# Feed-forward parts of 2, 2, 4, 4, 4 and 2 token tiles instead of 2, 2, 2, 3, 3, 3 and 3 in a planned attention, feed-forward and expert kernel

## The chip, the core and the metric

One core of a Trainium2 chip runs the whole program. The metric is the device time of one execution in microseconds (us). The kernel before takes 813.25 us (median of three runs, 813.02 to 813.59).

## What is computed

2304 tokens (18 tiles of 128) of width 512 go through three layers:

```python
scores = scale * q @ k.T                       # 4 batches, 8 heads, 576 positions, width 64
attn   = softmax(where(0 <= i - j < 64, scores, -1e9))
x      = attn @ v                              # 2304 x 512
xn     = x / sqrt(mean(x*x) + 1e-6) * rms_g
x      = (silu(xn @ w_gate) * (xn @ w_val)) @ w_out       # d_ff 1536
logits = x @ w_gate2;  e = argmax(logits)                 # 8 experts
out    = softmax(logits)[e] * sigmoid(x @ w_output_gate)[e] * (relu(x @ w1[e]) @ w2[e])
```

All is float32. The large products are made of three: each operand is split into a rounded high part and the rest, and high x high, high x low and low x high are added up in one PSUM bank.

## The kernel before

**Parts and groups.** `SIZES` cuts the 18 token tiles into feed-forward parts. Parts 0 and 1 form the first group and run side by side; every later part is a group of its own. A group goes through the 12 chunks of d_ff (`ffn_step`, L968 on): for one chunk and one part, 12 matmuls make the gate (`gv`, L993 to L995, into one bank of 128 x 128 times the number of tiles), 12 make the value, ScalarE takes tanh of the gate (L1005), VectorE makes u from it and multiplies with the value (L1010, L1018), h is split into high and low (helpers at L452 and L459), and `mo` (L1035 to L1037) adds three matmuls over 512 columns to the accumulator of each tile. So a part of n tiles holds n of the eight PSUM banks from its first chunk to its last. `ffn_end` copies the accumulators out (L1051, L1053).

**What runs beside it.** Before a group, the attention of its tiles must be done (`attention_tile`: scores L680 and L688, maximum L707, exponentials L717, transposes L751, product with v L768, norm L795 to L845); their normed tokens go to `xn`, a room in SBUF of six tiles' size that the parts share by the offsets in `XN_AT`. In the first group the weights are converted too (`conv`: three loads, three splits per chunk) and written back to `whd` in DRAM (`save`); every later group keeps the four chunks that the one before it used last and loads the other eight from `whd` (L969). The buffers of tag `w` hold one chunk each: four are there from the start, five more when attention is over, one when the feed-forward layer is over.

**Routing and the first expert.** Behind each part, `route` transposes its tokens (L1103), makes the logits (L1110, L1118), picks the expert and the slot of every token, and POOL scatters the tokens by slot to `xs` in DRAM (L1199). After the last part but one `plan_first` counts the tokens of each expert so far (matmul L1274) and picks the fullest; its number (`idf`) tells SP which weights to load (L1415, to `raw`, then split to `w`) and which two tiles of its tokens (L1452, to `t2k`). They are transposed (L1469) and are the first expert block, which fills the time in which the last part is routed. Then come the eight experts in order of size (`experts`).

**What sets the order.** Every operation is given to `Plan` with its engines, a cost and a due time; `Plan.order` hands them out in a list schedule, by due time plus the entry of `SHIFT` for its place, and keeps slots of buffers and banks. The result is a fixed order for each engine: each runs its queue in order, and waits at an instruction whose inputs are not there. `K` holds the planner's constants. Where the plan sees TensorE waiting at the start, it puts small matmuls on a spare bank (`warm`, L624).

Of the kernel before, what the change touches and what calls it, by code (L numbers as in the profile page):

```python
# [10 lines left out]
F32R = mybir.dt.float32r  # L11
# [11 lines left out]
P = 128  # L23
# [7 lines left out]
SIZES = [2, 2, 2, 3, 3, 3, 3]  # L31
GROUPS = [[0, 1], [2], [3], [4], [5], [6]]
XN_AT = [0, 2, 4, 0, 3, 0, 3]
# [4 lines left out]
K = dict(  # L38
    w_r=4, sl=1.2, n_q=4, n_kt=4, n_s=4, n_m=4, n_p=4, n_x=4, n_y=3, n_xf=1, n_val=3, pf=0.1, cold=6.0, late=1, f0=24.0, pw=110.0, pb=0.6, c1a=0, c1v=0, spe=4, lact=0, warm=62.816, wf=1.644, flead=24.233, nwv=1, port=1.0, t0=46.214, pp=93.267,
    lead=1.781, clead=9.978, stag=2.552, stage=1.001, slack=-0.04, nt=2, look=-0.072, marg=-0.199, dw=1.739, ewl=3.278,  # L40
    ews=8.339, xld=43.407, xtn=7.222, mlead=14.712, vb=0.333, vb2=0.243, tb=22.485, share=-0.055, pls=9, phs=9, sf=0, hfs=1.431, stk=0.0, rlead=7.936, span=0.317, wl=1.841,
)
# [45 lines left out]
]  # L88


class Buf:


    def __init__(self, tag=None, t=None):
        self.tag, self.t, self.slot = tag, t, None
        self.last_w, self.reads = {}, {}
# [278 lines left out]
def attention_ffn_moe(  # L375
# [21 lines left out]
    KD = DM // P  # L397
# [220 lines left out]
    warm = []  # L618
# [1193 lines left out]
```

## Time and profile before

| | |
|---|---|
| median of three runs | 813.25 us |
| the profiled execution | 815.9 us |
| its span, first to last instruction | 813.9 us |
| TensorE (PE) busy | 798.6 us, 98% |
| weight loads (PEld) busy | 723.1 us, 89% |
| VectorE (DVE) busy | 471.1 us, 58% |
| ScalarE (ACT) busy | 355.0 us, 44% |
| GpSimd (POOL) busy | 59.6 us, 7% |
| moved by DMA | 146.12 MB, mean 180 GB/s |
| granted TensorE clock, mean | 0.997 of full |

A group of the profile is one line of the kernel, one engine and one shape: its count, its busy time, the mean of one, and how long the engine sat idle before it and for whom. Matmuls are pipelined, so the mean of one is longer than the distance from one start to the next; the timeline gives the starts. SP issues the DMAs; it is a queue of its own.

### The profile page before, as it was taken

What the parts mean: (1) busy time and instruction counts of PE and PEld (TensorE: products, weight loads), DVE (VectorE), ACT (ScalarE), POOL (GpSimd) and SP (SyncE); (2) the same over time, 40 slices, a digit from 0 to 9 for tenths busy, and PEclk for the clock granted to TensorE, in tenths of its full rate; (3) what the DMA queues carried; (4) which work ended last, traced back from release to release, by engine and by line L of the source; (5) the groups of instructions that cost most, each with busy time, mean ns of one, the idle gap of its engine ahead of it and who ended that gap; (6) DMA issues with size and microseconds to landing.
All of it is one profiled execution on the core that took longest, in us unless ns stands there. A gap on an engine that the chain in (4) does not pass through costs nothing.

```text
span 813.9 us, 15811 instructions
## 1 busy us (share of the span) xinstructions
PE 798.6 (98%) x6050; PEld 723.1 (89%) x6050; DVE 471.1 (58%) x1262; ACT 355.0 (44%) x993; POOL 59.6 (7%) x103
## 2 busy tenths in 40 slices
PE   9999999999999999999999999999999999999995
PEld 8899998889999998899999999898988799988893
DVE  6999998774554433852445334355466574666650
ACT  6988767664333323631523122223245333534530
POOL 2110000020000010200100101000100100110010
PEclk9999999999999999999999999999999999999998
DMA  8888899977335501642044904710295562756420
GB/s 303 281 270 292 302 287 332 293 255 269 126 130 188 188 26 53 247 146 87 2 156 162 362 33 143 234 52 1 78 330 174 188 205 91 227 188 227 152 83 21
DMA packets 53933, 146.12 MB, mean 180 GB/s; under 512 B 6800, under 2 KB 6800, under 8 KB 53856
## 3 DMA queue, kind: packets, MB, share of 16 engines
q1 hardware_dynamic: 50848, 135.36, 49.4%
q0 software_dynamic: 3008, 9.74, 3.1%
q8 instruction: 48, 0.79, 0.4%
q14 instruction: 29, 0.24, 0.1%
HBM read 120.66 MB, written 24.42 MB: 178 GB/s over the span
## 4 chain that ended last, share of the span: by engine, by line
PE 78%; issue 9%; DMA 6%; DVE 4%; SPq 1%; ACT 1%; POOL 0%; POOLq 0%; ACTq 0%; DVEq 0%
PE bank L993 11%; PE bank L995 10%; PE bank L994 10%; PE bank L1035 5%; PE bank L1036 5%; PE bank L1037 5%; PE bank L1538 3%; PE bank L1540 3%; PE bank L1539 3%; DMA raw<-in_moe_w_dram 3%; PE bank L1630 3%; PE bank L1632 3%; PE bank L1631 3%; PE bank L768 2%; PE bank L751 2%
## 5 line engine op out<-in xcount | busy, mean ns | idle before, releaser
L993 PE MATMUL bank<-xn,w 128*128 128x384 f32 (+1 forms) x672 | 215.2, 320 | 1.3 <-DVE u L1010 1.3
L995 PE MATMUL bank<-xn,w 128*128 128x384 f32 (+1 forms) x672 | 210.2, 313 | 0.0
L994 PE MATMUL bank<-xn,w 128*128 128x384 f32 (+1 forms) x672 | 210.1, 313 | 0.0
L993 PEld LDWEIGHTS bank<-xn,w 128*128 128x128 f32 x672 | 127.2, 189 | 6.2 <-DVE u L1010 1.7
L994 PEld LDWEIGHTS bank<-xn,w 128*128 128x128 f32 x672 | 127.1, 189 | 1.7
L995 PEld LDWEIGHTS bank<-xn,w 128*128 128x128 f32 x672 | 126.9, 189 | 0.0
L1010 DVE SCALAR_TENSOR_TENSOR u<-u,bank 128x384 f32<-128x384 f32 (+1 forms) x84 | 41.4, 494 | 88.4 <-ACT u L1005 88.0
L459 DVE TENSOR_TENSOR w<-raw,w 128x512 fp32r<-128x512 f32 x128 | 81.8, 684 | 10.5 <-ACT w L452 10.2
L1035 PE MATMUL bank<-wo,h 128*128 128x512 f32 x216 | 86.5, 401 | 0.0
L1036 PE MATMUL bank<-wo,h 128*128 128x512 f32 x216 | 84.8, 393 | 0.0
L1037 PE MATMUL bank<-wo,h 128*128 128x512 f32 x216 | 84.8, 392 | 0.0
L1005 ACT ACTIVATE u<-bank 128x384 f32<-128x384 f32 (+1 forms) x84 | 37.4, 447 | 95.6 <-PE bank L995 94.1
L452 ACT CAST h<-u 128x384 fp32r<-128x384 f32 (+1 forms) x73 | 34.2, 468 | 97.3 <-DVE u L1018 93.5
L1018 DVE TENSOR_TENSOR u<-u,bank 128x384 f32<-128x384 f32 (+1 forms) x84 | 41.5, 494 | 55.0 <-PE bank L995 53.8
L1538 PE MATMUL bank<-xT,w 128*128 128x256 f32 (+4 forms) x224 | 68.0, 304 | 1.5 <-DVE eh L1549 1.5
L1540 PE MATMUL bank<-xT,w 128*128 128x256 f32 (+4 forms) x224 | 67.3, 300 | 0.0
L1539 PE MATMUL bank<-xT,w 128*128 128x256 f32 (+4 forms) x224 | 67.2, 300 | 0.0
L452 ACT CAST w<-raw 128x512 fp32r<-128x512 f32 x85 | 48.8, 620 | 40.4 <-DMA raw<-in_moe_w_dram 16.8
L1630 PE MATMUL bank<-w,eh 128*128 128x512 f32 (+1 forms) x144 | 57.3, 398 | 0.0
L1544 ACT ACTIVATE eh<-bank 128x256 fp32r<-128x256 f32 (+4 forms) x64 | 26.2, 411 | 70.1 <-PE bank L1540 68.1
L1632 PE MATMUL bank<-w,eh 128*128 128x512 f32 (+1 forms) x144 | 56.7, 394 | 0.0
L1631 PE MATMUL bank<-w,eh 128*128 128x512 f32 (+1 forms) x144 | 56.7, 394 | 0.0
(234 smaller groups left out, 1363.6 us busy)
## 6 DMA issues: line engine op xcount, KB each, us to landing
w<-whd SPq DMA_DIRECT2D x80, 512.0 KB, 4.3
raw<-in_moe_w_dram SPq DMA_DIRECT2D x64, 512.0 KB, 5.1
whd<-w SPq DMA_DIRECT2D x24, 512.0 KB, 6.8
val<-in_v_dram SPq DMA_DIRECT2D x18, 512.0 KB, 3.3
kt<-in_k_dram SPq DMA_DIRECT2D x18, 384.0 KB, 6.6
raw<-in_moe_w_gate_dram SPq DMA_DIRECT2D x12, 512.0 KB, 5.0
raw<-in_moe_w_val_dram SPq DMA_DIRECT2D x12, 512.0 KB, 5.4
raw<-in_moe_w_out_dram SPq DMA_DIRECT2D x12, 512.0 KB, 5.9
```

The source lines that it names most:

```text
L452: nc.scalar.copy(o, i)
L459: ve[e].tensor_tensor(out=o, in0=i, in1=h, op=ALU.subtract)
L993: nc.tensor.matmul(o, lhsT=h_, rhs=xn.t[:, 0, kk], start=(kk == 0), stop=False)
L994: nc.tensor.matmul(o, lhsT=h_, rhs=xn.t[:, 1, kk], start=False, stop=False)
L995: nc.tensor.matmul(o, lhsT=l_, rhs=xn.t[:, 0, kk], start=False, stop=(kk == KD - 1))
L1035: nc.tensor.matmul(o, lhsT=h.t[:, 0, c], rhs=wo.t[:, 0, f], start=(n == 0), stop=False)
L1036: nc.tensor.matmul(o, lhsT=h.t[:, 0, c], rhs=wo.t[:, 1, f], start=False, stop=False)
L1037: nc.tensor.matmul(o, lhsT=h.t[:, 1, c], rhs=wo.t[:, 0, f], start=False, stop=(n == NF - 1))
L1538: nc.tensor.matmul(o, lhsT=wh, rhs=x.t[:, 0, kk, 0:N], start=(kk == 0), stop=False)
L1539: nc.tensor.matmul(o, lhsT=wh, rhs=x.t[:, 1, kk, 0:N], start=False, stop=False)
L1540: nc.tensor.matmul(o, lhsT=wl, rhs=x.t[:, 0, kk, 0:N], start=False, stop=(kk == KD - 1))
L1630: nc.tensor.matmul(bk.t[0:M], lhsT=hh, rhs=wh, start=(f == 0), stop=False)
```

## The change

The parts become 2, 2, 4, 4, 4 and 2 tiles. `xn` has room for eight tiles, so a part of four can be read while the next part's four are written. Buffers that are as wide as a part (u, h, the routing's small tables) grow to four tiles. To make room, the attention has three buffers for k, not four; of the `w` buffers one that came when attention was over now comes when the feed-forward layer is over, and `pln`, the table of the last planning step, also comes then. The planner's constants and all of `SHIFT` are new, so that the order of every engine is new. The instructions of attention, of the output projection and of the experts are as many as before.

```diff
-SIZES = [2, 2, 2, 3, 3, 3, 3]
-GROUPS = [[0, 1], [2], [3], [4], [5], [6]]
-XN_AT = [0, 2, 4, 0, 3, 0, 3]
+SIZES = [2, 2, 4, 4, 4, 2]
+GROUPS = [[0, 1], [2], [3], [4], [5]]
+XN_AT = [0, 2, 4, 0, 4, 0]
...
-    w_r=4, sl=1.2, n_q=4, n_kt=4, n_s=4, n_m=4, n_p=4, n_x=4, n_y=3, n_xf=1, n_val=3, pf=0.1, cold=6.0, late=1, f0=24.0, pw=110.0, pb=0.6, c1a=0, c1v=0, spe=4, lact=0, warm=62.816, wf=1.644, flead=24.233, nwv=1, port=1.0, t0=46.214, pp=93.267,
-    lead=1.781, clead=9.978, stag=2.552, stage=1.001, slack=-0.04, nt=2, look=-0.072, marg=-0.199, dw=1.739, ewl=3.278,
-    ews=8.339, xld=43.407, xtn=7.222, mlead=14.712, vb=0.333, vb2=0.243, tb=22.485, share=-0.055, pls=9, phs=9, sf=0, hfs=1.431, stk=0.0, rlead=7.936, span=0.317, wl=1.841,
+    w_r=4, sl=1.2, n_q=4, n_kt=3, n_s=4, n_m=4, n_p=4, n_x=4, n_y=3, n_xf=1, n_val=3, pf=0.1, cold=6.0, late=1, f0=24.0, pw=110.0, pb=0.6, c1a=0, c1v=0, spe=4, lact=0, warm=50.376, wf=2.323, flead=24.233, nwv=1, port=1.0, t0=46.214, pp=93.267,
+    lead=1.781, clead=9.978, stag=2.552, stage=1.001, slack=0.09, nt=2, look=-0.944, marg=0.033, dw=1.502, ewl=3.278,
+    ews=8.339, xld=43.407, xtn=7.222, mlead=14.712, vb=0.26, vb2=0.734, tb=240.248, share=-0.025, pls=9, phs=9, sf=0, hfs=1.431, stk=0.053, rlead=7.936, span=0.317, wl=1.841,
...
-    27.9, 32.5, -30.4, -6.6, -30.9, -2.2, 14.9, -18.9, -29.4, -12.2, -14, -10.2, -17.3, 2.2, -8.6, -67.2, -20, -17.8, -1.6, 1.1, 15.8, 14.7, -22.3, 1.4,
+    -24.3, -39.7, -60.5, -75.7, -59.5, -9.2, -7.3, -36.3, -37.3, -23.9, -37.4, -1.9, -62.3, -24.9, -3.3, -8.4, 16.3, -40, -9.7, -14.7, -26.9, -2.8, -47.7, -76.8,
...
-    tag("w", [("r", K["w_r"]), ("mr", 9 - K["w_r"]), ("ml", 1)], 0, [P, 2, 2, KD, P], F32R)
+    tag("w", [("r", K["w_r"]), ("mr", 8 - K["w_r"]), ("ml", 2)], 0, [P, 2, 2, KD, P], F32R)
     tag("fx", "mr", 1, [P, 2, KD, FIRST * P], F32R)
-    tag("pln", "mr", 1, [1, 1024])
+    tag("pln", "ml", 1, [1, 1024])
...
-    xn_all = fp.tile([P, 6 * 2 * KD * P], F32R, name="xn", bufs=1)
+    xn_all = fp.tile([P, 8 * 2 * KD * P], F32R, name="xn", bufs=1)
```

Two lines fewer in the tables make every line of the functions two smaller: L993 before is L991 now.

**TensorE, inside a part of three tiles before and of four now.** The last three matmuls of a value group and the first three of the output projection, before:

```order
L993 MATMUL bank_3908<-xn,w_3808 128x384
L994 MATMUL bank_3908<-xn,w_3808 128x384
L995 MATMUL bank_3908<-xn,w_3808 128x384
L1035 MATMUL bank_3818<-wo,h_3874 128x512
L1036 MATMUL bank_3818<-wo,h_3874 128x512
L1037 MATMUL bank_3818<-wo,h_3874 128x512
```

and now:

```order
L991 MATMUL bank_3415<-xn,w_3152 128x512
L992 MATMUL bank_3415<-xn,w_3152 128x512
L993 MATMUL bank_3415<-xn,w_3152 128x512
L1033 MATMUL bank_3333<-wo,h_3382 128x512
L1034 MATMUL bank_3333<-wo,h_3382 128x512
L1035 MATMUL bank_3333<-wo,h_3382 128x512
```

Each gate or value matmul streams 512 columns where it streamed 384; over all parts these lines have 576 matmuls each instead of 672, 288 of them over 512 columns. The warm-up matmuls of L624 are 258 instead of 248.

**TensorE, where the tokens of the first expert block (`t2k`) are transposed.** Before, behind the last output matmuls of the last part:

```order
L1035 MATMUL bank_6366<-wo,h_6908 128x512
L1036 MATMUL bank_6366<-wo,h_6908 128x512
L1037 MATMUL bank_6366<-wo,h_6908 128x512
L1469 MATMUL bank_6944<-ident,t2k_6568 128x128 x4
L1469 MATMUL bank_6954<-ident,t2k_6547 128x128 x4
L1103 MATMUL bank_6961<-ident,raw_6950 128x128 x4
L1103 MATMUL bank_6971<-ident,raw_6952 128x128 x4
```

and now, inside the last part:

```order
L1033 MATMUL bank_5896<-wo,h_6270 128x512
L1034 MATMUL bank_5896<-wo,h_6270 128x512
L1035 MATMUL bank_5896<-wo,h_6270 128x512
L1467 MATMUL bank_6348<-ident,t2k_6285 128x128 x4
L991 MATMUL bank_6356<-xn,w_5873 128x256
L992 MATMUL bank_6356<-xn,w_5873 128x256
L993 MATMUL bank_6356<-xn,w_5873 128x256
```

The transposes of the first tile moved from behind the last chunk to a place with nine gate and value groups of the part behind them. Between the count (L1274 before, L1272 now) and this place the new order has 96 gate and value matmuls over 256 columns and 24 output matmuls.

**SP, the first loads for the first expert block.** `raw` are weights, `t2k` tokens. Before:

```order
L1392 TENSOR_LOAD idf
L1415 ISA
L1415 DMA raw_6539<-in_moe_w_dram 128x2x512
L1392 TENSOR_LOAD idf
L1452 ISA
L1452 DMA t2k_6547<-xs 128x514
L1415 ISA
L1415 DMA raw_6566<-in_moe_w_dram 128x2x512
L1392 TENSOR_LOAD idf
L1452 ISA
L1452 DMA t2k_6568<-xs 128x514
```

and now:

```order
L1413 DMA raw_6239<-in_moe_w_dram 128x2x512
L1413 ISA
L1413 DMA raw_6251<-in_moe_w_dram 128x2x512
L1413 ISA
L1413 DMA raw_6267<-in_moe_w_dram 128x2x512
L1390 TENSOR_LOAD idf
L1450 ISA
L1450 DMA t2k_6285<-xs 128x514
L1390 TENSOR_LOAD idf
L1450 ISA
L1450 DMA t2k_6306<-xs 128x514
```

Three weight loads stand ahead of the first token load where one stood. VectorE's first weight cast of this block reads the third load now (`raw_6267`), the fifth before, and stands with four steps of the last part to come, not six.

## Rows read from the trace of the kernel before

**Rows 1.** The page: span, TensorE's share, and the granted clock in 40 slices.
```profile
span 813.9 us, 15811 instructions
...
PE 798.6 (98%) x6050; PEld 723.1 (89%) x6050; DVE 471.1 (58%) x1262; ACT 355.0 (44%) x993; POOL 59.6 (7%) x103
...
PEclk9999999999999999999999999999999999999998
```

**Rows 2.** TensorE's waits: operation <- releaser: us in total, times, longest.
```profile
PE bank L1538 <- DVE eh L1549: 1.5, 2, 1.1
PE bank L993 <- DVE u L1010: 1.3, 1, 1.3
PE warm L624 <- DVE ones_b L535: 1.2, 1, 1.2
```

**Rows 3.** The timeline, TensorE, the last matmul: start, us.
```profile
804.60 0.40 PE L1632 MATMUL bank<-w,eh 128*64 128x512 f32 x1
```

**Rows 4.** TensorE's groups by shape: count, busy us, mean ns, idle before.
```profile
L993 PE MATMUL bank<-xn,w 128*128 128x384 f32 x384 | 131.5, 342 | 1.3 <-DVE u L1010 1.3
...
L624 PE MATMUL warm<-ones_b 128*128 128x128 bf16 x248 | 18.5, 234 | 1.2 <-DVE ones_b L535 1.2
```

**Rows 5.** The timeline, TensorE: first and next start of four runs of matmuls.
```profile
61.93 0.28 PE L993 MATMUL bank<-xn,w 128*128 128x256 f32 x1
...
64.81 1.03 PE L751 MATMUL bank<-ident,s 128*128 128x128 f32 x8
...
250.30 0.33 PE L993 MATMUL bank<-xn,w 128*128 128x384 f32 x1
...
254.49 1.03 PE L1103 MATMUL bank<-ident,raw 128*128 128x128 f32 x8
...
543.77 0.40 PE L1035 MATMUL bank<-wo,h 128*128 128x512 f32 x1
...
547.89 0.34 PE L993 MATMUL bank<-xn,w 128*128 128x384 f32 x1
...
777.63 0.39 PE L1631 MATMUL bank<-w,eh 128*128 128x512 f32 x1
...
782.99 0.25 PE L1538 MATMUL bank<-xT,w 128*128 128x192 f32 x1
```

**Rows 6.** The page's DMA issues: the weight reloads, KB each, us to landing.
```profile
w<-whd SPq DMA_DIRECT2D x80, 512.0 KB, 4.3
```

**Rows 7.** Busy time by stretch: length, PE, PEld, DVE, ACT, POOL, clock, DMA share, GB/s.
```profile
46.00:100.00 54.00, 53.84 (x460) 49.95 (x459) 50.67 (x127) 45.27 (x118) 2.08 (x2) 1.00 0.87 285
100.00:160.00 60.00, 60.00 (x515) 54.88 (x513) 52.19 (x128) 40.34 (x108) 1.04 (x1) 1.00 0.96 302
...
200.00:300.00 100.00, 100.00 (x728) 92.30 (x726) 47.02 (x127) 34.47 (x114) 3.14 (x5) 1.00 0.41 146
```

**Rows 8.** VectorE's and ScalarE's groups: four that come with every attention tile.
```profile
L707 DVE TENSOR_REDUCE m<-bank 128x4 f32<-128x512 f32 x36 | 23.5, 681 | 6.1 <-PE bank L688 6.1
...
L717 ACT ACTIVATE s<-bank,m 128x128 f32<-128x128 f32 x144 | 50.9, 379 | 0.5
...
L717 ACT ACTIVATION_READ_ACCUMULATOR s<-bank,m 128x1 f32 x144 | 31.6, 219 | 0.0
...
L452 ACT COPY p<-bank 128x512 f32<-128x512 f32 x30 | 17.2, 591 | 11.4 <-PE bank L751 11.2
```

**Rows 9.** The timeline, 500 to 530 us: count, scatters, loads, first cast.
```profile
502.45 0.18 PE L1274 MATMUL bank<-pf,ones_b 128*128 128x8 bf16 x1
...
504.52 0.97 POOL L1199 DMA_INDIRECT xs<-raw,si  x1 [48.42 <-issue]
...
505.80 0.98 POOL L1199 DMA_INDIRECT xs<-raw,si  x1 [0.22 <-issue]
...
512.54 0.40 SPq L1415 DMA_DIRECT2D raw<-in_moe_w_dram  x1
513.56 0.35 SPq L1452 DMA_DIRECT2D t2k<-xs  x1
...
517.93 0.15 DVE L1462 COPY meta<-t2k 128x1 int32<-128x1 int32 x1 [1.51 <-DMA t2k<-xs]
...
526.49 0.43 DVE L456 CAST w<-raw 128x512 fp32r<-128x512 f32 x1 [3.14 <-DMA raw<-in_moe_w_dram]
```

80 rows, old and new, of the table SHIFT are left out of this document.

## The prediction

> **What bounds the kernel.** I read the page's first two parts, then TensorE's own waits, then its groups by shape, then its pace in the timeline, then the stretches in which another engine could stop it. The profiled execution took 815.9 us, its span 813.9 us; the median of the runs is 813.25 us, 2.65 us less. The sum below is made against 815.9 and then moved by that 2.65.
>
> In [rows 1] TensorE (PE) is busy for 98% of the span and its granted clock stands at 9 tenths or more in every slice but the last. In [rows 2] everything that ever stopped it for over 1 us is 1.5 us in the expert blocks (L1538, two waits), 1.3 us in the last feed-forward part (L993, one wait) and the start (L624). The last matmul starts at 804.60 us [rows 3]; the 9.3 us behind it are the last output tile and stay. So the time is the number of matmuls times their pace, plus stalls. A change of the parts pays only if TensorE streams its columns in less time, or waits less.
>
> **The change, part by part.**
>
> *Gate and value matmuls.* The three-tile parts issue 1152 matmuls over 384 columns, 384 on each of three lines [rows 4]. The change issues 864 over 512 columns: three parts of four tiles, 12 chunks, 2 x 12 matmuls each. The busy means there (342 ns) overlap, so the price is the distance of starts [rows 5]. At 384 columns 24 matmuls take 254.49 - 250.30 = 4.19 us, 0.1746 each; 1152 of them are 201.1 us. At 512 columns there is none of this line, but the output projection has that shape: 18 from 543.77 to 547.89 give 0.2289, and the expert layer's 23 from 777.63 to 782.99 give 0.2330. 864 of them are 197.8 to 201.3 us; I take the middle, 199.6 (0.231 each). **Gain 1.5 us, between 3.3 us and a loss of 0.2 us.** The gain is small because 384 and 512 columns cost 0.455 and 0.451 ns a column. The Trainium skill (TensorE: Matmul & The Clock Gate, section "Back-to-back issue gap") gives columns over 2.4 GHz plus about 2.5 ns for a matmul. By it I estimate 187.2 us for the old and 186.5 us for the new, a gain of 0.7 us. The rows are 12 to 17 ns above that rule at the two widths, so the measured paces stand. The output projection (648 matmuls) and the 864 matmuls at 256 columns stay as many.
>
> *Warm-up matmuls.* 248 now, 258 then; 18.5 us over 248 is 0.075 us each [rows 4], so 10 more are 0.75 us if they lengthen the start, 0 if they stand in a wait that is there anyway. The order places them only while TensorE waits for the first attention tiles. I take +0.4, bounds 0 and +0.75.
>
> *One part fewer.* 72 steps, not 84, on VectorE and ScalarE, and one routing round fewer: beside TensorE's matmuls, so nothing, whatever it saves.
>
> *Weight reloads.* 80 becomes 64 loads of 512 KB [rows 6]. They run in stretches where the DMA engines are busy for 0.41 of the time [rows 7]; nothing waits for them, so their loss brings nothing. If that cover went, one costs 4.3 us to land.
>
> *Two attention tiles more beside the first group.* The part behind the first group has four tiles, not two, so two tiles move from later into the weight conversion. TensorE's work for them is only moved. VectorE and ScalarE are the danger: from 46 to 160 us they are busy for 102.9 and 85.6 of 114 us, and TensorE still idles for only 0.16 us of them [rows 7]. A tile brings them at least 6.8 us: the four groups of [rows 8] are 123.2 us over 18 tiles. Two tiles are 13.7 us into 39.5 us of free time of the two engines. It fits, if it is spread; if it all fell on one engine half of it, 6.9 us, could show. Nearest row: the idle 0.16 us at that load. I take +0.4, bounds 0 and +6.9. Their loads (q, k, v) are also pulled forward, into DMA shares of 0.87 and 0.96 [rows 7]; that is in the same bound.
>
> *The last part and the first expert block.* Here the order moves most. Before, the last part has 12 steps of three tiles; the expert that goes first is counted early in it (matmul L1274, 502.45 us), SP then loads weights and tokens, and VectorE's first weight cast waits for its load until 526.49 us, 24.0 us after the count [rows 9]. VectorE runs in order; the u operation of the next step is queued behind that cast, and this is the 1.3 us of [rows 2]. That wait is tied to that place, which is gone: **-1.3 us** (bounds -1.3 and 0).
>
> In its place: in the new order PE comes to the first transpose of the first block's tokens inside the last part, with steps still behind it, where it stood after the last step. Between the count and that transpose stand 8 groups of 12 at 256 columns and four half-steps of 6 output matmuls; with 0.120 us (24 from 61.93 to 64.81, [rows 5]) and 0.231 us that is 11.5 + 5.5 = 17.0 us. The tokens come through the chain count, slot numbers, scatter on POOL, its landing, SP's load. Before, the first token tile is there at 517.93 us, 15.5 us after the count [rows 9]. In the new order three weight loads stand ahead of it on SP, not one; a place is 512.54 to 513.56 = 1.02 us, so +2.0. Four tiles are scattered, not three; one is 504.52 to 505.80 = 1.28 us, hidden or not. It lands 17.5 to 18.8 us after the count, 0.5 to 1.8 us after TensorE wants it; all steps left wait behind it in TensorE's queue. I take **+1.2 us**, bounds 0 (TensorE itself late) and +7.0 (the 24.0 us of the cast, less 17.0).
>
> *The rest planned anew.* The 1.5 us in the expert blocks are a matter of the order; 0, bounds -1.5 and +1.5.
>
> **Sum:** -1.5 + 0.4 + 0.4 - 1.3 + 1.2 + 0 = -0.8 us: 815.1 us for the profiled execution, **812.4 us** for the median. A difference under 0.2% (1.6 us) cannot be told from none by a measurement of this kernel.
>
> **Rivals.**
> 1. *Faster, 808 us.* The pace comes out at its lower bound, and the new order meets neither the old waits nor the new one: -3.3 + 0 + 0 - 1.3 + 0 - 1.5 = -6.1 us, 807.2 us. For it: 512 columns at 0.2289 are in the rows. Against: the other 512-column row is 0.2330, and the tokens' chain is measured. 0.20, for 807 to 811.
> 2. *Slower: the last part waits for the first expert block.* Place: the token transpose and the first weight cast in the last part. Price: from 3 to 7 us above the sum. It decides when the first token tile lands later than 20 us after the count, or the first cast holds VectorE with the u and h operations behind it (7 groups and 18 output matmuls, 14.3 us, stand between the count and that place). For it: the cast took 24.0 us before. Against: it then waited for the fifth weight load, now for the third. 815.4 to 819.4 us, 0.18.
> 3. *Slower: the first group runs out of VectorE and ScalarE*, up to 6.9 us, 816 to 819 us. 0.08; the rows speak for room.
> 4. *The clock falls.* With four accumulators TensorE has only four banks left to turn over in three parts. In the trace the first group already works so, and the granted clock is 1.00 there, 2.4 GHz [rows 7]. At 1.2 GHz every wide matmul would take 0.46 instead of 0.23 us, so 30 us at that level cost 15 us: 828 us. The Trainium skill (same page, section "A second HAM failure mode: psum-queue depth-cycling") tells of a kernel whose cycling through banks made the clock swing. By that rule the time would be that of this rival; the trace disagrees so far. 0.02.
> 5. *The start gets shorter*, 809 to 811 us, by some of the 18.5 us of warm-up. Against it: there are more of them, not fewer. 0.04.
>
> **How the numbers follow.** The forecast has 0.48, as 811.0 to 814.0 us; about 0.11 of that is below 811.6. Faster: 0.11 + 0.20 + 0.04 = 0.35. Within 0.2%: 0.37. Slower: 0.18 + 0.08 + 0.02 = 0.28. The range 808.5 to 818.5 us cuts a part of rival 1 and the top of rivals 2 and 3, and leaves out rival 4.
>
> **What would show it.** Right: 288 matmuls over 512 columns on each gate and value line, 24 of them in 5.5 to 5.6 us; no wait on L993 behind a weight cast over 1 us; a wait on the token transpose in the last part of 0.5 to 2 us on DMA; PE 98% busy. Wrong if TensorE idles by over 3 us in the last part (rival 2), or waits for u or a weight in the first group (rival 3), or if PEclk shows a slice under 9 (rival 4); and the pace is wrong if 24 wide matmuls take less than 5.4 us or more than 5.7 us.

## The result, and the profile after

The changed kernel takes 805.06 us (median of five runs, 804.04 to 807.94) where the kernel before takes 813.25: ratio 0.9898, 95% interval 0.9877 to 0.9918. It is faster by 8.2 us, 1.0%; the prediction was 812.4 us, and its range began at 808.5. Its profiled execution took 805.13 us, its span 803.3. Later comparisons gave 0.988 and 0.989.

The page of the changed kernel, first two parts:

```profile
span 803.3 us, 15138 instructions
...
PE 790.4 (98%) x5770; PEld 685.6 (85%) x5770; DVE 444.4 (55%) x1158; ACT 368.1 (46%) x1004; POOL 71.6 (9%) x117
...
PEclk9999999999999999999999999999999999999998
```

Beside [rows 1] the share of TensorE is the same 98% and the clock is as high; what fell is the busy time itself. The kernel was bound by TensorE and still is; it has less to stream. Its last matmul starts at 793.88 us (804.60 in [rows 3]), so the 9.4 us behind it are what they were, and all of the gain lies ahead of it.

TensorE's groups by shape and its longest waits:

```profile
L991 PE MATMUL bank<-xn,w 128*128 128x512 f32 x288 | 115.3, 400 | 0.0
...
L991 PE MATMUL bank<-xn,w 128*128 128x256 f32 x288 | 83.2, 289 | 0.6 <-DVE u L1016 0.6
...
L622 PE MATMUL warm<-ones_b 128*128 128x128 bf16 x258 | 19.3, 233 | 1.2 <-DVE ones_b L533 1.2
```

```profile
PE warm L622 <- DVE ones_b L533: 1.2, 1, 1.2
PE bank L843 <- DVE m L727: 1.1, 1, 1.1
PE bank L991 <- DVE u L1016: 0.6, 1, 0.6
```

The 288 wide matmuls a line are there. Of the two long waits of [rows 2], the expert layer's is gone and the last part's is shorter. The timeline of TensorE inside a part of four tiles, first matmul of a group and the start 24 matmuls later, and the last matmul of all:

```profile
196.38 0.39 PE L991 MATMUL bank<-xn,w 128*128 128x512 f32 x1
...
201.82 0.39 PE L991 MATMUL bank<-xn,w 128*128 128x512 f32 x1
...
793.88 0.40 PE L1630 MATMUL bank<-w,eh 128*64 128x512 f32 x1
```

24 matmuls (12 of a gate, 12 of a value) in 5.44 us: 0.2267 us each, where the prediction took 0.231 and named 5.5 to 5.6 us as the sign of being right. Of its other signs, the 98% came and no wait stands behind a weight cast; the wait on the token transpose did not come.

Where the time went is best seen by adding up, over a whole trace, the distance from each matmul's start to the next one's, shape by shape. A distance up to 45 ns above the median of its shape I count whole as streaming. Of a longer one the median counts as streaming and the rest as a hitch (45 to 130 ns over the median) or a wait (more). What the hitches are the traces do not tell. In us:

| trace | streaming | hitches | waits | sum |
|---|---|---|---|---|
| before | 750.7 | 33.3 | 19.4 | 803.4 |
| before, second trace | 750.9 | 33.5 | 17.9 | 802.3 |
| changed | 745.7 | 31.7 | 15.3 | 792.7 |
| changed, second trace | 745.1 | 32.8 | 15.3 | 793.2 |
| changed, third trace | 745.7 | 32.2 | 14.6 | 792.4 |

Streaming repeats within 0.6 us from one execution to the next. Means of these rows: 5.3 us less streaming, 1.2 less in hitches, 3.6 less in waits, 10.1 in all (the executions traced of before, 815.9 and 814.7 us, lie 2.65 and 1.45 us above the median of 813.25, so this is 1.9 more than the 8.2 of the medians). Of the streaming, the wide gate and value matmuls gave 3.5 (200.6 to 197.1), the output projection, whose instructions did not change, 1.3 (149.3 to 148.0), the second expert matmuls 0.6 (99.8 to 99.2).

### The profile page after: what moved, and what is told of

Read it like the earlier page. It is cut to its first block, busy times and chain, and to the rows that moved or that the text cites. A ratio compares the mean times of both kernels' runs of the same rounds, so it can differ in the third digit from the quotient of the medians.

```text
span 803.3 us, 15138 instructions
## 1 busy us (share of the span) xinstructions
PE 790.4 (98%) x5770; PEld 685.6 (85%) x5770; DVE 444.4 (55%) x1158; ACT 368.1 (46%) x1004; POOL 71.6 (9%) x117
## 5 line engine op out<-in xcount | busy, mean ns | idle before, releaser
L991 PE MATMUL bank<-xn,w 128*128 128x256 f32 (+1 forms) x576 | 198.5, 345 | 0.6 <-DVE u L1016 0.6
L993 PE MATMUL bank<-xn,w 128*128 128x256 f32 (+1 forms) x576 | 193.9, 337 | 0.0
L992 PE MATMUL bank<-xn,w 128*128 128x256 f32 (+1 forms) x576 | 193.7, 336 | 0.0
L991 PEld LDWEIGHTS bank<-xn,w 128*128 128x128 f32 x576 | 109.0, 189 | 14.1 <-issue 0.8
L993 PEld LDWEIGHTS bank<-xn,w 128*128 128x128 f32 x576 | 108.9, 189 | 11.7
L992 PEld LDWEIGHTS bank<-xn,w 128*128 128x128 f32 x576 | 109.1, 189 | 11.2
L1008 DVE SCALAR_TENSOR_TENSOR u<-u,bank 128x256 f32<-128x256 f32 (+1 forms) x72 | 39.5, 550 | 89.1 <-ACT u L1003 88.8
L450 ACT CAST h<-u 128x512 fp32r<-128x512 f32 (+1 forms) x65 | 34.0, 522 | 105.4 <-DVE u L1016 104.9
L1016 DVE TENSOR_TENSOR u<-u,bank 128x256 f32<-128x256 f32 (+1 forms) x72 | 39.7, 551 | 74.2 <-PE bank L993 73.1
L1003 ACT ACTIVATE u<-bank 128x256 f32<-128x256 f32 (+1 forms) x72 | 35.4, 492 | 96.5 <-PE bank L993 95.6
L450 ACT CAST w<-raw 128x512 fp32r<-128x512 f32 x99 | 56.2, 619 | 23.7 <-DMA raw<-in_moe_w_dram 11.8
L457 DVE TENSOR_TENSOR h<-u,h 128x256 fp32r<-128x256 f32 (+1 forms) x72 | 40.4, 561 | 23.9 <-ACT h L450 23.4
```

The source lines that it names most:

```text
L450: nc.scalar.copy(o, i)
L457: ve[e].tensor_tensor(out=o, in0=i, in1=h, op=ALU.subtract)
L991: nc.tensor.matmul(o, lhsT=h_, rhs=xn.t[:, 0, kk], start=(kk == 0), stop=False)
L992: nc.tensor.matmul(o, lhsT=h_, rhs=xn.t[:, 1, kk], start=False, stop=False)
L993: nc.tensor.matmul(o, lhsT=l_, rhs=xn.t[:, 0, kk], start=False, stop=(kk == KD - 1))
```

## The experiments

Each stands beside runs of the kernel before on the same chip.

**Both kernels once more.** No edit.

> The kernel before, unchanged, profiled once more. If the waits of its first trace belong to its order, the two longest (1.47 us on the gate matmul in the last part, 1.25 us on the expert weights) come again within 0.3 us, and all waits of TensorE over 0.13 us add up to 18 to 20 us. If they were chance of that execution (its 815.9 us stood 2.65 us over the median), one of the two is gone, the sum is 16 to 18 us and the span 811 to 812 us. The output matmuls over 512 columns: 0.231 us again if their pace is a matter of the kernel, 0.227 if of the execution.

> The changed kernel, unchanged, profiled and timed once more. If its gain is a matter of the kernel: ratio 0.988 to 0.992, 24 gate matmuls over 512 columns in 5.4 to 5.5 us, waits over 0.13 us of 15 to 16 us in all, no wait on the token transpose of the last part. If the first trace was a lucky one: a ratio over 0.993 and more waits.

Measured: before 814.7 us (span 812.8); changed 805.71, ratio 0.9884 (0.9851 to 0.9917). TensorE's waits in the second trace of before, and then of the changed kernel:

```profile
PE bank L993 <- DVE u L1010: 0.9, 1, 0.9
...
PE bank L1538 <- DVE eh L1549: 0.2, 1, 0.2
```

```profile
PE warm L622 <- DVE ones_b L533: 1.2, 1, 1.2
PE bank L1033 <- ACT h L450: 1.2, 1, 1.2
```

Of the two longest waits of [rows 2], the one behind the weight cast (1.3 us) is 0.9 us now and the one in the expert blocks (1.5 us) is 0.2: partly chance. And the changed kernel has a wait in its last part too, now on the output matmul (1.2 us, and 1.3 in the third trace; the gate wait of 0.6 us above is not there). TensorE waits there for h, and VectorE, which makes u for it, had waited 3.1 us for ScalarE's tanh. ScalarE's timeline at this tanh, first and second trace of the changed kernel:

```profile
530.22 0.38 ACT L1003 ACTIVATE u<-bank 128x256 f32<-128x256 f32 x1 [1.12 <-PE bank L993]
```

```profile
532.09 0.38 ACT L1003 ACTIVATE u<-bank 128x256 f32<-128x256 f32 x1 [3.14 <-PE bank L993]
```

The gate matmuls that it reads ended at 530.12 and 529.97 us. So the tanh followed after 0.1 us in one execution and after 2.1 us in the other, in the same order; why is not shown. Both median paces of the output matmuls, 0.231 and 0.227, came again: they belong to the kernels.

**The parts alone, in an order that nobody shaped.** `SHIFT` emptied in both, so that the planner's own order stands.

```diff
-SHIFT = [ -24.3, ...
+SHIFT = []
-    n_q=4
+    n_q=3
 # and, in parts3_plain alone
-SIZES = [2, 2, 4, 4, 4, 2]
+SIZES = [2, 2, 2, 3, 3, 3, 3]
-XN_AT = [0, 2, 4, 0, 4, 0]
+XN_AT = [0, 2, 4, 0, 3, 0, 3]
```

> The changed kernel with its table of shifts emptied (the planner's own order) and three q buffers, not four, so that its buffers fit. To be set against parts3_plain, which differs from it in the parts alone. Theory A (a fixed cost per matmul, so 288 fewer matmuls are worth something in any order): the 864 matmuls over 512 columns start 0.227 us apart, 3 to 4 us less in all than the 1152 over 384 columns of the other. Rival B (the order chosen by the shifts gives the pace): 0.231 us apart, and no difference of over 1 us in these matmuls. In both the waits grow, so the whole is 815 to 850 us; the sum of waits says how much of that is the order's.

> The same as parts4_plain (changed kernel's planner constants and buffers, room for eight tiles, table of shifts emptied, three q buffers), but with the parts of before: 2, 2, 2, 3, 3, 3, 3. Theory A: its gate and value matmuls over 384 columns take 0.173 to 0.175 us each, 200 to 201 us for 1152 without waits, 3 to 4 us more than the wide ones; output matmuls 0.229 to 0.231. Rival B: no difference of over 1 us. If it takes fewer waits than parts4_plain, the wide parts need the new order to be worth their gain; then the two times differ by less than 3 us or the other way round.

Measured: parts of four 817.86 us, ratio 1.0038 (1.0022 to 1.0054); parts of three 822.26, ratio 1.0093 (1.006 to 1.0127): 4.4 us apart.

| trace | streaming | hitches | waits | sum |
|---|---|---|---|---|
| parts3_plain | 755.1 | 31.5 | 22.7 | 809.4 |
| parts4_plain | 750.0 | 31.7 | 24.5 | 806.2 |

The difference in streaming is 5.1 us, nearly the 5.3 between the two kernels: gate and value 200.7 to 197.1, output 149.7 to 148.3. Theory A holds and the rival with the order falls. The wide parts do not wait less by themselves (1.8 us more here); that leaves the order for the fewer waits of the changed kernel.

**The wide matmuls cut in two.** The changed kernel, each gate and value group of a four-tile part done in two halves of 256 columns.

```diff
+            for c in (slice(0, 2 * P), slice(2 * P, 4 * P))[:PT // 2]:
             for kk in range(KD):
-                o = bk.t[:, 0:TW]
-                nc.tensor.matmul(o, lhsT=h_, rhs=xn.t[:, 0, kk], ...
+                o = bk.t[:, c]
+                nc.tensor.matmul(o, lhsT=h_, rhs=xn.t[:, 0, kk, c], ...
```

> The changed kernel, same parts and same order, but every gate or value matmul over 512 columns is issued as two over 256 (first all 12 of the left half, then all 12 of the right). Theory A (a fixed cost of 13 to 14 ns per matmul above columns over 2.4 GHz): 1728 matmuls at 0.1195 us are 206.5 us where the 864 took 197.1, so 9.4 us more. Theory A2 on the output matmuls (512 columns, unchanged): the first ones behind narrower matmuls are slower, 232 ns, and come down to 227 ns only from about the tenth on; so their mean in these parts goes from 227.4 to about 230 ns, 1.1 us more. Together 814 to 817 us. Rival: the pace of the output matmuls hangs on the parts of four tiles (banks, buffers), then it stays 227.4, and the whole is 814 to 815.

Measured: 814.67 us, ratio 1.002 (1.001 to 1.0031): the whole gain is gone, and a little more. Streaming is 756.2 us. 2592 matmuls over 256 columns take 310.1 where the mix took 300.2 (197.05 + 103.18): 9.9 us for 864 more instructions on the same columns, 11.4 ns each. Each of these matmuls has a weight load of its own; which of the two costs this, no run separates. The waits fell to 12.9 us, perhaps because a slower TensorE hides more. The timeline, TensorE, an output run behind the narrow matmuls, every third start:

```profile
298.61 0.40 PE L1034 MATMUL bank<-wo,h 128*128 128x512 f32 x1
...
299.31 0.39 PE L1034 MATMUL bank<-wo,h 128*128 128x512 f32 x1
...
300.00 0.39 PE L1034 MATMUL bank<-wo,h 128*128 128x512 f32 x1
...
300.68 0.39 PE L1034 MATMUL bank<-wo,h 128*128 128x512 f32 x1
```

And the same in the second trace of before, behind matmuls over 384 columns:

```profile
262.06 0.39 PE L1035 MATMUL bank<-wo,h 128*128 128x512 f32 x1
...
262.76 0.39 PE L1035 MATMUL bank<-wo,h 128*128 128x512 f32 x1
...
263.45 0.39 PE L1035 MATMUL bank<-wo,h 128*128 128x512 f32 x1
...
264.14 0.39 PE L1035 MATMUL bank<-wo,h 128*128 128x512 f32 x1
...
264.82 0.39 PE L1035 MATMUL bank<-wo,h 128*128 128x512 f32 x1
```

Three take 0.70 us at first, then 0.69, and from the seventh (behind 256 columns) or tenth (behind 384) matmul of the run on 0.68: 0.233 each comes down to 0.227. In the changed kernel, behind matmuls over 512 columns, it is 0.68 from the first start on:

```profile
190.94 0.39 PE L1033 MATMUL bank<-wo,h 128*128 128x512 f32 x1
...
191.62 0.39 PE L1033 MATMUL bank<-wo,h 128*128 128x512 f32 x1
...
192.30 0.39 PE L1033 MATMUL bank<-wo,h 128*128 128x512 f32 x1
```

Theory A2 is right in kind. In size it is not: the output matmuls took only 0.3 us more in all, not 1.1 (148.35 against 148.0), since behind 256 columns they settle after six. Why they start slow the traces do not tell.

**The token load made later.** The changed kernel; on SP six weight loads ahead of the first token load, not three.

```diff
 raw<-in_moe_w_dram x3
+raw<-in_moe_w_dram x3
 t2k<-xs x2
-raw<-in_moe_w_dram x3
```

> The changed kernel with three more weight loads ahead of the first token load on SP (six where three stood), nothing else moved. This doubles the cost that the prediction put at +1.2 us. In the trace of the changed kernel the token tile is there some 1.5 us before TensorE comes to it. If three loads cost 1.0 us each on SP and as much again on the DMA engines, it lands 3 to 5 us later, TensorE waits 1.5 to 3.5 us on the token transpose or on the steps behind the token copy on VectorE, and the time is 806 to 809 us. If SP or the DMA engines have more room than that: no wait, 804.5 to 806 us.

Measured: 809.81 us, ratio 0.9964 (0.9948 to 0.998). The changed kernel was not run beside it; against its ratios of 0.988 to 0.990 this is 5 to 7 us more, by the sums over the traces (797.3 against 792.8) 4.5. The wait, and the timeline of TensorE and VectorE at that place:

```profile
PE bank L1467 <- DMA t2k<-xs: 3.9, 1, 3.9
```

```profile
545.08 1.00 PE L1467 MATMUL bank<-ident,t2k 128*128 128x128 f32 x4 [3.94 <-DMA t2k<-xs]
...
544.97 0.15 DVE L1460 COPY meta<-t2k 128x1 int32<-128x1 int32 x1 [4.16 <-DMA t2k<-xs]
```

So the wait that the prediction feared is a real mechanism, and it costs its full length and more: when the wait ends, TensorE's granted clock is 0.50 (1.2 GHz) from 545.2 to 548.6 us, and matmuls over 256 columns start 0.213 us apart there, 0.120 afterwards. Busy time by stretch, columns as in [rows 7], and starts six matmuls apart at the lower clock and afterwards:

```profile
545.20:548.60 3.40, 3.40 (x17) 3.40 (x17) 1.39 (x4) 0.58 (x1) 0.00 (x0) 0.50 0.43 135
```

```profile
546.30 0.41 PE L993 MATMUL bank<-xn,w 128*128 128x256 f32 x1
...
547.58 0.41 PE L993 MATMUL bank<-xn,w 128*128 128x256 f32 x1
...
549.10 0.28 PE L993 MATMUL bank<-xn,w 128*128 128x256 f32 x1
...
549.82 0.28 PE L993 MATMUL bank<-xn,w 128*128 128x256 f32 x1
```

What I had wrong is the wait's cause. SP issued the token load at 537.43 us, only 1.3 us later than in the changed kernel; it then took 7.4 us to land, not 3.6, behind six weight loads instead of three. DMA issues between 525 and 545 us, of the changed kernel and of this one (KB each, median us from issue to landing):

```profile
t2k<-xs SPq DMA_DIRECT2D x2, 257.0 KB, 3.6
```

```profile
t2k<-xs SPq DMA_DIRECT2D x2, 257.0 KB, 7.4
```

**The old cast wait taken away.** The kernel before; on VectorE the next u operation goes ahead of the first weight cast.

```diff
+L1010 SCALAR_TENSOR_TENSOR u<-u,bank 128x384
 L456 CAST w<-raw 128x512
 L459 TENSOR_TENSOR w<-raw,w 128x512 x2
-L1010 SCALAR_TENSOR_TENSOR u<-u,bank 128x384
```

> The kernel before with one u operation of VectorE put ahead of the first weight cast of the expert block (and the two operations on that weight), all else as it was. The prediction counted the wait on this cast as -1.3 us. If it is worth that, the wait of 1.0 to 1.5 us on the gate matmul in the last part is gone, no other wait of over 0.5 us comes in its place in that part, and the span is 811.5 to 812.5 us. If the wait only moves (the next u or h operation stands behind the cast instead), the sum of waits in the last part stays within 0.3 us of the first one's.

Measured: 815.42 us in one run, span 813.6 (the kernel before there: median 813.04). The waits of the last part, and ScalarE's timeline there:

```profile
PE bank L993 <- DVE u L1010: 0.6, 1, 0.6
...
PE bank L993 <- DVE u L1018: 0.3, 1, 0.3
```

```profile
526.39 1.14 ACT L452 CAST w<-raw 128x512 fp32r<-128x512 f32 x2 [2.85 <-DMA raw<-in_moe_w_dram]
527.44 0.48 ACT L1005 ACTIVATE u<-bank 128x384 f32<-128x384 f32 x1
```

0.9 us became 0.6 + 0.3. The tanh that u needs stands behind another weight cast, on ScalarE, and that waits for a weight load too; all of TensorE's waits come to 18.2 us, between the two traces of before. By moving the one cast the term of 1.3 us was not to be had.

**One step further: 4, 4, 4, 4 and 2.** The first group one part of four, first in the planner's own order, then twice with tables of shifts made for it.

```diff
-SIZES = [2, 2, 4, 4, 4, 2]
+SIZES = [4, 4, 4, 4, 2]
-GROUPS = [[0, 1], [2], [3], [4], [5]]
+GROUPS = [[0], [1], [2], [3], [4]]
-XN_AT = [0, 2, 4, 0, 4, 0]
+XN_AT = [0, 4, 0, 4, 0]
```

> Parts of 4, 4, 4, 4 and 2 tiles (the first group one part of four, not two parts of two), the changed kernel's planner constants, table of shifts emptied, three q buffers; to be set against parts4_plain at 817.86 us. Theory A: 288 matmuls over 512 columns take the place of 576 over 256, 65.4 for 68.8 us, and 144 output matmuls go from 231.5 to 227.5 ns: 4.0 us less of TensorE's streaming whatever the order. With the same waits 814 us. Rival: a single part has nothing to put between gate, u, h and output in the first group, and the waits grow by more than 4 us: 818 us or more.

> Parts of 4, 4, 4, 4 and 2 tiles again, now with a table of shifts and planner constants of its own, three q buffers. Theory A: TensorE's streaming falls by 2.3 us against the changed kernel, as it did between parts4_plain and parts44442 (750.0 to 747.7 us), to 742.5 to 743.5 us; if the order waits as little as the changed kernel's (15 to 16 us over 0.13 us), the time is 801.5 to 804 us, faster than both kernels. Rival: a single part in the first group leaves TensorE nothing beside it, the waits come to 18 us or more, and the time is 805 to 808 us.

> The same parts as p44442_a with another table of shifts and other constants. Streaming within 0.5 us of p44442_a, whatever the order; the two times differ by their waits alone. 801.5 to 805 us by theory A, 805 to 808 us by the rival.

Measured: in the planner's own order 814.38 us, ratio 1.002 (1.0006 to 1.0033), on another chip than parts4_plain (817.86, 1.0038), so 3.5 us less by the medians and 1.5 by the ratios; with tables of its own 804.37 and 803.71, ratios 0.9886 (0.987 to 0.9903) and 0.9881 (0.9864 to 0.9897).

| trace | streaming | hitches | waits | sum |
|---|---|---|---|---|
| parts44442 | 747.8 | 32.5 | 24.5 | 804.7 |
| p44442_a | 744.2 | 31.7 | 15.7 | 791.6 |
| p44442_b | 744.7 | 31.3 | 15.0 | 791.0 |

From parts4_plain to parts44442 streaming fell by 2.3 us (750.0 to 747.8 in the tables), not 4.0: the gate and value matmuls gave 3.0 (300.2 to 297.2), the output projection 0.6, scores and norm of the attention 1.7, and 54 more warm-up matmuls took 3.0 back. With an order of its own only 0.4 to 1.5 us are left against the changed kernel; 282 and 280 warm-up matmuls stand there, not 258, and take up to 1.4 us more. Whether it is faster at all was asked once more:

> The changed kernel, unchanged, in five rounds on the same chip as p44442_5: 804.5 to 806 us, and streaming of TensorE within 0.7 us of its two earlier traces.

> The kernel of p44442_b, unchanged, in five rounds on the same chip as after_5. If its 1.3 us against the changed kernel are real: 0.8 to 2.0 us less than after_5. If they were chance: within 0.5 us of it or slower.

Measured on the same chip: changed kernel 805.59 us, ratio 0.989 (0.9873 to 0.9907); 4, 4, 4, 4, 2 805.09, ratio 0.9876 (0.986 to 0.9891). 0.5 us apart, and the intervals overlap: no gain is shown. Its trace has waits of 1.49 us in the last part and 1.08 us at the first expert block.

## Why the prediction was wrong

The mechanism was right: TensorE bounds the kernel, and the time is columns, instructions and waits. The way was that of rival 1, at 0.20, but the time fell below its 807 us too: it had the pace and the order at the ends of their bounds, and nothing for the instructions that stay. Term by term:

1. **Gate and value matmuls** (said -1.5, between -3.3 and +0.2; measured -3.3 over all distances, -3.5 of streaming). The step that failed is "I take the middle": by streaming the 864 wide matmuls cost 197.1 us, not 199.6, and the old 1152 cost 200.6, not 201.1. The output projection's 0.2289 was a mean over a run whose first nine start slow; its last nine were at 0.2267 (2.04 us). The expert layer's 0.2330 was another pace: that run does not come down at all (nine starts late in it take 2.11 us, 0.234 each), and the whole expert layer stays at 0.232 a matmul before and 0.230 after; why is not shown. In the trace before, 15 starts of the gate's run of [rows 5] and nine of each of these two runs:

```profile
251.37 0.33 PE L993 MATMUL bank<-xn,w 128*128 128x384 f32 x1
...
253.97 0.33 PE L993 MATMUL bank<-xn,w 128*128 128x384 f32 x1
...
545.62 0.39 PE L1037 MATMUL bank<-wo,h 128*128 128x512 f32 x1
...
547.66 0.39 PE L1037 MATMUL bank<-wo,h 128*128 128x512 f32 x1
...
780.19 0.40 PE L1630 MATMUL bank<-w,eh 128*128 128x512 f32 x1
...
782.30 0.39 PE L1630 MATMUL bank<-w,eh 128*128 128x512 f32 x1
```

Widths that the gate's line did hold would have given it too: 0.120 at 256 columns and 0.1733 at 384 (2.60 us over 15) are columns over 2.4 GHz, the clock granted there, plus some 13 ns, and at 512 that is 213.3 + 13 = 226 ns. A line through two widths beat two means at the right width. The Trainium skill (TensorE: Matmul & The Clock Gate, section "Back-to-back issue gap") puts the gap of an isolated matmul at columns over 2.4 GHz plus about 2.5 ns. The trace disagrees, with 13 ns in this stream; by the rule I estimate 0.7 us for 288 fewer matmuls, measured were 3.5.
2. **The output projection and the experts** (said 0 for work that stays as it is). The prediction gave no reason why their pace should stay. They gave 1.3 and 0.6 us of streaming: behind wide matmuls the output's slow start is gone. An unchanged instruction changed its pace with its neighbours. That the output's 1.3 us belong to the parts is shown by the plain pair (149.7 to 148.3); the experts' 0.6 did not come in that pair (99.9 and 100.0), so it is not the parts'.
3. **Warm-up** (+0.4): 13.9 us of streaming before, 14.4 after: right. With the waits among them it is 17.6 and 17.4 us before, 18.4, 17.5 and 16.7 after.
4. **Two attention tiles more in the first group** (+0.4; said 13.7 us of work for VectorE and ScalarE). The work came as worked out: busy time from 46 to 160 us rose by 4.1 us on VectorE and 10.0 on ScalarE against [rows 7], 14.1 in all. TensorE idled 0.20 us there, not 0.16. The cover held and the term is 0. Busy time by stretch, columns as in [rows 7]:

```profile
46.00:100.00 54.00, 53.80 (x518) 49.53 (x517) 51.55 (x135) 50.32 (x142) 3.29 (x4) 1.00 0.82 288
100.00:160.00 60.00, 60.00 (x530) 55.51 (x529) 55.42 (x138) 45.26 (x121) 2.79 (x3) 1.00 0.92 290
```

5. **The old cast wait** (-1.3). Wrong as a term: a wait of 0.6 to 1.3 us on VectorE's or ScalarE's results is in the last part of all three traces of the changed kernel, and in before_u_first the old one only moved.
6. **The token wait** (+1.2). The timelines of the changed kernel:

```profile
524.20 0.17 PE L1272 MATMUL bank<-pf,ones_b 128*128 128x8 bf16 x1
...
529.85 3.79 SPq L1413 DMA_DIRECT2D raw<-in_moe_w_dram  x3
536.11 1.25 SPq L1450 DMA_DIRECT2D t2k<-xs  x2
...
541.25 0.60 PE L1467 MATMUL bank<-ident,t2k 128*128 128x128 f32 x4
```

TensorE came 17.05 us after the count; the working said 17.0. But the tile was there after 536.11 + 3.6 - 524.20 = 15.5 us, as before, not 17.5 to 18.8. The step that failed is "three weight loads stand ahead of it on SP, not one, so +2.0": it added them to an old start. The first weight load went out 5.7 us after the count, not 10.1, and what held the token load was not the weight loads but the scatters. SP's own waits between 525 and 540 us:

```profile
SPq L1413 <- DMA xs<-raw,si: 3.6, 3, 1.5
SPq L1450 <- DMA xs<-raw,si: 1.9, 1, 1.9
```

SP waits 3.6 us for scatters at the weight loads and 1.9 us more at the token load, until the last scatter (started on POOL at 530.32) lands at 536.0 us, 0.1 us before the token load goes out: the three weight loads stand in time that SP waits anyway. late_tokens shows that the margin of about 1.5 us (15.5 against 17.05) is all there is.
7. **The rest planned anew** (0, between -1.5 and +1.5). Waits fell by 3.6 us and hitches by 1.2, with the cast wait among them. The plain pair shows that this is not the parts, which leaves the order. That it would be better could not be read from the trace of before; that 19 us of waits stood in it could, and a bound of 1.5 us for them was too narrow.

So the streaming, about 5 us, was there to be predicted; the remaining 3 to 5 us, put down to the order, were open to either side. The range failed because the middle of two rows, one with a slow start and one of another pace, stood for a price, and zeros stood for terms that had not been bounded below.

## What to carry to other kernels

On a kernel that TensorE bounds, count matmul instructions as well as columns: here each, with its weight load, cost 11 to 13 ns beyond its columns, so one over 512 columns cost less than two over 256. Price a shape from the steady part of a run, or from a line through two widths, and not from the mean of a short run behind another shape, nor from another line's run of the same width. When a step is moved, rebuild its whole chain from the event that starts it and look for what releases each link (here the last scatter); adding the new steps to the old finish charges for time that the new order may have won earlier.

## What was not expected of the hardware

- Output matmuls over 512 columns start 0.233 us apart behind narrower ones and 0.227 from the seventh or tenth on; behind others over 512 columns they are at 0.227 at once. The expert layer's of the same shape run at 0.230 to 0.232 on the mean, in some runs with no settling.
- The streaming of one program repeats within 0.6 us of 750 from execution to execution; what varies by 1 to 2 us are waits.
- A load that was issued 1.3 us later landed 5.2 us later (537.43 + 7.4 against 536.11 + 3.6): three more 512 KB loads ahead of it doubled its time under way.
- After the idle 3.9 us in late_tokens TensorE's granted clock was 0.50 from 545.2 to 548.6 us; with the same place unbroken it was 1.00. Some 16 matmuls took 0.09 us more each, an estimate of 1.5 us from the two paces above.
